# Linear attention gated by a SwiGLU block, one core: the split of the output weights in another stage, the exponentials' stores on another queue, and VectorE's scaling kept apart from GpSimd's products

## The chip, the cores and the metric

The kernel runs on one core of a Trainium2 chip. The time is the device time of one execution in microseconds (us). Three runs of the kernel before took 2455.68, 2459.19 and 2461.28 us, so the median is 2459.19 us. TensorE (PE) multiplies matrices out of SBUF into PSUM, VectorE (DVE) and ScalarE (ACT) work element by element on both memories, and GpSimd (POOL) does so on SBUF. SyncE (SP) issues the DMAs of the kernel before; each engine works through its own queue in order and waits there on semaphores.

## The reference

With x of 2048 tokens by 1024 (32 heads of 32), all in float32:

```python
xn = _layernorm(x)
# linear attention with a learned feature map
q, k, v = (xn @ wqkv), split into heads
pq, pk  = q @ w_phi, k @ w_phi                       # per head, 32 x 32
phi_q   = concat(softmax(pq), softmax(-pq))          # 64 features per head
phi_k   = concat(softmax(pk), softmax(-pk))
kv = phi_k^T v;  z = sum over tokens of phi_k
o  = (phi_q kv) / (phi_q z + 1e-6)
s  = o @ wo
# SwiGLU, 1024 -> 3584 -> 1024
g  = silu((silu(xn @ w1) * (xn @ w3)) @ w2)
out = x + s * g
```

## The kernel before, in words

Each float32 operand of a large product is split into two float32r tiles: `hi` is a cast of the source on ScalarE, `lo` is source minus `hi` on VectorE or GpSimd (`split`, L90 to L93). A product is three passes over such pairs (`PASSES`). The large products also use a seven-product scheme (`ORDER`): a pair of token tiles of 128 is taken together, and seven products of twelve matmuls each (128x128 by 128x512) give four blocks of the result; the sums of blocks that it needs are the operands A11, A12, S1 to S4, A22 for tokens and B11 to T4 for weights.

The span has these stages, with their times in the profile:

1. **Gate and up, 0 to 1141 us.** Two halves of the tokens (`tb`), 28 chunks of 128 columns of w1 and w3 each; one chunk takes about 19 us, the second half begins at about 599 us. The order of all engines is written out by hand here: `at(step, f)` puts a piece of work at a step. Beside the products of the second half the kernel prepares later weights: sums of w2's blocks (`side_w`, tile `w2o`) and the split of wo (`side_split`, L503 to L514, called at L567 to L569). wo is cut into 16 blocks of 128x512; for each, SP loads the block (256 KB), ScalarE casts, **GpSimd** subtracts (tile `wso`), and SP stores the pair to `wo_d` (512 KB).
2. **Queries, 1141 to about 1304 us** (`query_heads` L865, `query_features` L848). Eight pairs of tiles. Seven products at L874, then per tile the feature map: maximum and minimum, subtraction, and the exponential on ScalarE into one of two rooms `eq` (`e_rooms`). Each room holds both halves `c` of a tile; a half (128x1024, 512 KB) is stored to `e_d` at L863, **from SP**: four stores per pair, 32 in all. The sums give `rho` (the weights 1/sum), stored at L899.
3. **Keys and values, 1304 to 1655 us** (`heads` L800, for `c` = 1 and 2, eight pairs each). Seven products per pair at L810. ScalarE copies results out of the banks (L816 `k`, L823 and L831 `ev`), then the exponentials and kv matmuls follow. `room_ev` takes the tile `ev` from the same pool and tag (`rw`) as the two `eq` rooms: the first `ev` needs a room whose last store to `e_d` has landed. Before this stage SP also fetches the weights' sums (`fetch` L167: `op3T`, `op3B`; 2 MB each) and reloads the tokens' operands for the next pair (`reload`, L579: `xoA`, `xoS`; 512 KB each).
4. **Down-projection, 1655 to 2206 us** (`product` L1122). Seven blocks `kb` of the inner dimension by eight pairs; about 9.5 us per pair. In the last block (`kb` = 6) each finished pair also gets silu (`gate`) and its store, and the exponentials of the first tiles are loaded back (`load_e` L1079) and prepared for the last stage.
5. **Last stage, 2206 to 2454 us**, 16 tiles `t` of 128 tokens. Here too the order on all engines is that of the code. Names: `ez` = exponentials times z (`z_products` L1090, GpSimd, two halves of 128x1024); `z_sums` sums them per head (L1098, VectorE, 128x1024 to 128x32, twice) and multiplies by the weights `rho` (L1099, 128x64); `add_pairs` adds across partitions with a small matmul `us` (L1105); `factors` is the reciprocal (L1111) and a multiplication by `rho` (L1112, 128x64); `scale` multiplies the exponentials by the factors (L1119, 128x1024, per half `c`) and transposes them (L1120). Then `attend` (64 small matmuls `po`, L1252), the cast and the subtraction to `oT` (L1257, L1258), `out_half` (24 matmuls `pm` with wo, L1267, per half), and `gated` (times g on VectorE L1275, plus x on GpSimd L1276). All the small 128x64 results lie in one tile `own`, in different columns for each tile `t` (`part_of`).

Outside of the stages with a written order, and for SP in the first six blocks of stage 4, a scheduler orders the instructions by their dependences and its own priorities, so a line's place in the code doesn't fix its place in the queue.

Of the kernel before, what the change touches and what calls it, by code (L numbers as in the profile page):

```python
# [8 lines left out]
F = mybir.dt.float32  # L9
R = mybir.dt.float32r  # L10
# [7 lines left out]
P = 128  # L18
# [11 lines left out]
def tile_kernel(ctx: ExitStack, tc: tile.TileContext, x, wkT, wqT, wv, wphi, wo, w1, w3, w2, out):  # L30
# [472 lines left out]
    def side_split(d, src, s0):  # L503

        def load():
            nc.sync.dma_start(blk2(15), src)

        def do():
            t = qp.tile([P, 2, 512], R, name="wso", tag="q")
            split(t[:, 0], t[:, 1], blk2(15), nc.gpsimd)  # L510
            at(s0 + 6, lambda: nc.sync.dma_start(d, t.bitcast(F)))

        at(s0, load)
        at(s0 + 4, do)  # L514

# [332 lines left out]
    def query_features(i, j, c, p, rho, eng):  # L848
# [14 lines left out]
        nc.sync.dma_start(e_d[pairs[i][j]][:, c], ef)  # L863
# [116 lines left out]

    NEXT = ({0: 2, 1: 3, 2: 4, 3: 5, 4: 6}, {0: 2, 1: 3, 2: 4, 3: 5, 6: 6}, {})
    for c in range(3):
# [5 lines left out]
        for pos, i in enumerate(order):  # L988
            nxt, end = {}, pos + 1 == len(pairs)

            def steps():
                for j in range(7):
# [12 lines left out]
                    yield  # L1005
# [76 lines left out]
    def part_of(t, m):  # L1082
        at_ = 128 + 256 * (t % 3) + 64 * m
        return own[:, at_:at_ + 64]

    def z_products(t):
        if t >= NT:
            return
        for c in range(2):
            nc.gpsimd.tensor_mul(ezs[c].rearrange("p (g n) -> p g n", g=2), e_slab(t)[:, c].rearrange("p (g n) -> p g n", g=2),  # L1090
                                 zb[:, c * 512:c * 512 + 512].unsqueeze(1).to_broadcast([P, 2, 512]))

    def z_sums(t):
        if t >= NT:
            return
        z = part_of(t, 0)
        for c in range(2):
            nc.vector.tensor_reduce(z[:, 32 * c:32 * c + 32], ezs[c].rearrange("p (n f) -> p n f", f=DH), axis=AX.X, op=OP.add)  # L1098
        nc.vector.tensor_mul(*(v.rearrange("p (c g h) -> p c g h", c=2, g=2) for v in (z, z)), w_all[:, t])  # L1099

    def add_pairs(t, tag):
        if t >= NT:
            return
        us[t] = ps.tile([P, 512], F, name="us", tag=tag, bufs=1)[:, :64]
        nc.tensor.matmul(us[t], own[:, :P], part_of(t, 0), start=True, stop=True)  # L1105

    def factors(t):
        if t >= NT:
            return
        r, by = part_of(t, 1), part_of(t, 2)  # L1110
        nc.vector.reciprocal(r, us.pop(t))  # L1111
        nc.vector.tensor_mul(*(v.rearrange("p (c g h) -> p c g h", c=2, g=2) for v in (by, r)), w_all[:, t])  # L1112

    def scale(t, c):
        if t >= NT:
            return
        e = e_slab(t)[:, c]
        e3 = e.rearrange("p (n f) -> p n f", f=DH)
        nc.vector.tensor_mul(e3, e3, part_of(t, 2)[:, 32 * c:32 * c + 32].unsqueeze(2).to_broadcast([P, H, DH]))  # L1119
        nc.vector.transpose(et_slab(t, c), e)  # L1120
# [29 lines left out]
    FIRST = ("A11", "A12", "S2")  # L1150
    old, banks, first, second = None, {}, ready[0], None
    for r, new in enumerate(steps):
# [14 lines left out]
        for b, an, bn in TURN:  # L1167
# [26 lines left out]
        if end:  # L1194
# [7 lines left out]
            elif i == 1:  # L1202
                load_e(0)
            elif i == 2:
                load_e(1)
                z_products(0)
            elif i == 3:
                z_sums(0)
                add_pairs(0, "kv")
                z_products(1)  # L1210
            elif i == 4:
                factors(0)
                z_sums(1)
                scale(0, 0)
            elif i == 5:
                add_pairs(1, "kv")
                scale(0, 1)
                load_e(2)
            elif i == 6:
                factors(1)  # L1220
                scale(1, 0)
                load_e(3)
            elif i == 7:
                z_products(2)
# [60 lines left out]
    prev, lows = None, []  # L1285
    for t in range(NT):
        load_e(t + 4)
        p = out_half(t, 0)
# [4 lines left out]
        z_sums(t + 2)  # L1293
        z_products(t + 3)
        scale(t + 1, 1)
        gated(t, 0, p, t + 1 == NT)
        store_out(t, 0)
        add_pairs(t + 2, "us")
        lows = [attend(t + 1, 0)]
        factors(t + 2)  # L1300
        scale(t + 2, 0)
        prev = out_half(t, 1, lambda: lows.append(attend(t + 1, 1)))
        for do in lows:
            if do:
                do()
# [42 lines left out]
```

## Time and profile before

The profiled execution took 2455.37 us, with a span of 2453.6 us; the median of the runs is 2459.19 us. One execution is described by the trace; PE's granted clock was full in most of the span (0.988 on average).

| Engine | Busy, us | Share of the span |
|---|---|---|
| PE (matmuls) | 2373.6 | 97% |
| PE (weight loads, beside the matmuls) | 1941.4 | 79% |
| VectorE | 1837.6 | 75% |
| ScalarE | 854.8 | 35% |
| GpSimd | 268.5 | 11% |

PE waits for nothing in most of the span. Its gaps are in few places, and these are found by the waits of PE and by windows over stages. A row of the windows gives the stretch, its length, and for each engine the busy time with the number of instructions in brackets; then PE's granted clock, the share of the DMA engines that were busy, and the GB/s that they moved. A row of the timeline gives the start, the time, the engine, the line and what was written from what; in brackets stand the idle time of the engine before it and what ended it. A row of waits gives who waited for whom: total, times, the longest.

### The profile page before, as it was taken

The page shows a single profiled execution, that of the slowest core. Times are in us where ns is not written, and L with a number is a line of the kernel's source. Part 1 is how long each engine was busy: PE and PEld are TensorE (multiplying, and loading weights), DVE is VectorE, ACT ScalarE, POOL GpSimd, SP SyncE. Part 2 cuts the span into 40 slices and gives each one's busy share as a digit, 9 for nine tenths or more (in the row PEclk, how much of TensorE's full clock was granted, in tenths as well). Part 3 has the DMA queues.
Part 4 walks back from the last instruction along what each step waited for, and adds up shares of the span by engine and source line. Part 5 has one row for each costly group of instructions (what it writes and reads, how often), then busy time and mean ns, then how long its engine had stood idle before and what let it go on. Part 6 is the DMA issues. An engine that isn't in the chain of part 4 may idle for free.

```text
span 2453.6 us, 37229 instructions
## 1 busy us (share of the span) xinstructions
PE 2373.6 (97%) x14354; PEld 1941.4 (79%) x14354; DVE 1837.6 (75%) x2795; ACT 854.8 (35%) x1501; POOL 268.5 (11%) x233
## 2 busy tenths in 40 slices
PE   7999999999999999999997999999999999988998
PEld 6888888888888887887876888888888888766777
DVE  8877787765788888864775555575788887687996
ACT  6445454443455555532221111124322222230000
POOL 1000000000000000001331000000111111233542
PEclk9999999999999999999998999999999999998999
DMA  5446799976898988857898758644444334559662
GB/s 211 147 156 206 259 358 343 322 251 204 289 333 310 338 298 320 291 196 281 326 350 346 244 178 330 208 147 165 172 180 172 125 107 172 167 176 292 185 174 95
DMA packets 287697, 578.00 MB, mean 236 GB/s; under 512 B 24208, under 2 KB 140064, under 8 KB 284832
## 3 DMA queue, kind: packets, MB, share of 16 engines
q1 hardware_dynamic: 287520, 575.63, 68.2%
q8 instruction: 113, 1.85, 0.3%
q14 instruction: 64, 0.52, 0.1%
HBM read 370.54 MB, written 205.00 MB: 235 GB/s over the span
## 4 chain that ended last, share of the span: by engine, by line
PE 77%; DVE 12%; DMA 6%; issue 3%; ACT 1%; POOL 0%; SPq 0%; DVEq 0%; POOLq 0%; ACTq 0%
PE bankb L614 21%; PE bankb L1133 11%; PE bankc L614 10%; PE bankb L810 7%; PE bankc L1133 6%; PE banka L614 5%; PE bankc L810 3%; PE bankb L874 3%; PE banka L1133 3%; DVE acc L1119 2%; PE banka L810 2%; PE bankc L874 1%; PE pm L1267 1%; DVE own L1098 1%; DVE bo L93 1%
## 5 line engine op out<-in xcount | busy, mean ns | idle before, releaser
L93 DVE TENSOR_TENSOR bo<-rw,bo 128x512 fp32r<-128x512 f32 x336 | 234.2, 699 | 154.9 <-ACT bo L92 154.3
L92 ACT CAST bo<-rw 128x512 fp32r<-128x512 f32 x336 | 206.5, 618 | 8.4 <-DVE bo L93 2.6
L1133 PE MATMUL bankb<-bo,as 128*128 128x512 f32 x816 | 200.9, 389 | 0.0
L1133 PEld LDWEIGHTS bankb<-bo,as 128*128 128x128 f32 x816 | 153.2, 188 | 31.8
L614 PE MATMUL bankb<-op0S,bo 128*128 128x512 f32 x672 | 163.0, 391 | 1.9 <-ACT op0S L92 1.2
L1267 PE MATMUL pm<-wos,oT 128*128 128x512 f32 x576 | 145.3, 402 | 18.7 <-DVE oT L1258 16.1
L614 PE MATMUL bankc<-op0S,bo 128*128 128x512 f32 x672 | 162.5, 391 | 0.3 <-DVE op0S L93 0.3
L614 PE MATMUL bankb<-op1S,bo 128*128 128x512 f32 x672 | 161.4, 389 | 1.3 <-ACT u L649 1.3
L614 PE MATMUL bankb<-op1A,bo 128*128 128x512 f32 x672 | 158.8, 391 | 3.5 <-DVE u L657 3.1
L614 PE MATMUL bankc<-op1S,bo 128*128 128x512 f32 x672 | 161.3, 389 | 0.0
L614 PE MATMUL bankb<-op0A,bo 128*128 128x512 f32 x672 | 159.7, 391 | 0.8 <-DVE bo L93 0.5
L614 PEld LDWEIGHTS bankb<-op1A,bo 128*128 128x128 f32 x672 | 125.2, 188 | 34.0 <-DVE u L657 8.4
L1133 PE MATMUL bankc<-bo,as 128*128 128x512 f32 x576 | 150.2, 396 | 0.8 <-ACT as L92 0.7
L614 PEld LDWEIGHTS bankb<-op1S,bo 128*128 128x128 f32 x672 | 126.1, 188 | 27.9 <-ACT u L649 1.8
L614 PEld LDWEIGHTS bankb<-op0S,bo 128*128 128x128 f32 x672 | 125.2, 188 | 28.5 <-ACT op0S L92 1.6
L614 PEld LDWEIGHTS bankc<-op1S,bo 128*128 128x128 f32 x672 | 126.1, 188 | 26.2
L614 PEld LDWEIGHTS bankb<-op0A,bo 128*128 128x128 f32 x672 | 125.2, 188 | 26.9 <-DVE bo L93 0.8
L614 PEld LDWEIGHTS bankc<-op0S,bo 128*128 128x128 f32 x672 | 125.3, 188 | 26.3 <-DVE op0S L93 0.7
L1267 PEld LDWEIGHTS pm<-wos,oT 128*128 128x128 f32 x576 | 107.1, 191 | 48.8 <-DVE oT L1258 21.8
L1133 PEld LDWEIGHTS bankc<-bo,as 128*128 128x128 f32 x576 | 109.6, 191 | 25.4 <-ACT as L92 2.0
L93 POOL TENSOR_TENSOR wso<-room,wso 128x512 fp32r<-128x512 f32 x16 | 24.2, 1512 | 961.4 <-ACT wso L92 845.0
L1145 DVE TENSOR_TENSOR acc<-bankb,acc 128x512 f32<-128x512 f32 x152 | 104.1, 686 | 27.0 <-PE bankb L1133 19.8
(249 smaller groups left out, 4489.2 us busy)
## 6 DMA issues: line engine op xcount, KB each, us to landing
rw<-in_w SPq DMA_DIRECT2D x112, 512.0 KB, 4.6
hr<-h_d SPq DMA_DIRECT2D x56, 512.0 KB, 3.5
h_d<-h SPq DMA_DIRECT2D x111, 256.0 KB, 4.7
xoS<-xo_d0S SPq DMA_DIRECT2D x44, 512.0 KB, 4.9
xoS<-xo_d1S SPq DMA_DIRECT2D x44, 512.0 KB, 6.8
xoA<-xo_d0A SPq DMA_DIRECT2D x33, 512.0 KB, 3.8
xoA<-xo_d1A SPq DMA_DIRECT2D x33, 512.0 KB, 5.9
e_d<-eq SPq DMA_DIRECT2D x32, 512.0 KB, 9.2
```

Source lines behind the costliest of these rows:

```text
L92: nc.scalar.copy(hi, src)
L93: (by or nc.vector).tensor_sub(lo, src, hi.bitcast(F))
L614: nc.tensor.matmul(bank[b], bos[tb, f][bn][:, w, k], ao[an][:, u, k], start=first and n == 0, stop=LAST[b] == an and n == 11, skip_group_c ...
L810: nc.tensor.matmul(bank[b], xo[an][:, u, k], wb[bn][:, w, k], start=an in ("A11", "A12", "S1") and n == 0, stop=LAST[b] == an and n == 11, ...
L874: nc.tensor.matmul(bank[b], xo[an][:, u, k], wb[bn][:, w, k], start=an in ("A11", "A12", "S1") and n == 0, stop=LAST[b] == an and n == 11, ...
L1098: nc.vector.tensor_reduce(z[:, 32 * c:32 * c + 32], ezs[c].rearrange("p (n f) -> p n f", f=DH), axis=AX.X, op=OP.add)
L1119: nc.vector.tensor_mul(e3, e3, part_of(t, 2)[:, 32 * c:32 * c + 32].unsqueeze(2).to_broadcast([P, H, DH]))
L1133: nc.tensor.matmul(bank[b], t[:, u, pos + k], bos[kb, bn, k][:, w], start=first and n == 0, stop=LAST[b] == an and n == 5, skip_group_chec ...
L1145: nc.vector.tensor_add(c, pb, c)
L1267: nc.tensor.matmul(p, oTs[t, h][:, a, k], wos[c, 4 * h + k][:, b], start=n == 0, stop=n == 3 * ND - 1)
```

## The change

The change has three parts.

**1. The split of wo is moved** from the second half of gate and up to the keys and values. `side_split` and its 16 calls are gone. `wo_split(c, k, j, halves)` is called in `steps` for `c` = 1 and 2, once per pair and product `j`: at `j` = 0 SP loads the block into a tile of the pool `work`, at `j` = 3 ScalarE casts and **VectorE** subtracts into two more, and at `j` = 5 SP stores the two halves (256 KB each).

**2. The stores of the exponentials to `e_d`** are issued by ScalarE's queue, right behind the exponential that they store, and no more by SP.

**3. The last stage.** The 128x64 multiplications by `rho` (`weigh`, before in `z_sums`; and the second half of `factors`) go from VectorE to GpSimd. Both write to one shared column of `own`, `col(0)`, which `scale` reads: so `weigh(t + 2)` on GpSimd waits until both halves of `scale(t + 1)` on VectorE have read it, and GpSimd's `z_products(t + 3)`, queued behind, waits with it. Both halves of `scale` stand together, and both transpositions (`turn_e`) behind them. The sums of `z_sums` are separate for each half and stand behind the two subtractions to `oT`. In the last block of the down-projection a table, `pieces`, keyed by pair and product, says where the preparation of the first tiles stands; `scale(1)` and its transpositions now belong to the last stage altogether (before, its first half was done in stage 4).

How this moves instructions is seen at the end of the queries and in the last stage. SP's queue at the end of the queries (`rho_d` ends a pair; `xoA` and `xoS` are the tokens' operands for the keys; `op3T` and `op3B` the keys' weights), before:

```order
L863 DMA e_d_235<-eq 128x1024
L899 DMA rho_d<-rho 128x2x32
L167 DMA op3T_10878<-wkv_d1T_110 128x4096
L863 DMA e_d_232<-eq 128x1024
L167 DMA op3T_10905<-wkv_d1T_111 128x4096
L167 DMA op3T_10921<-wkv_d1T_112 128x4096
L167 DMA op3B_10938<-wkv_d1B_113 128x4096
L863 DMA e_d_236<-eq 128x1024
L167 DMA op3T_10964<-wkv_d1T_114 128x4096
L863 DMA e_d_232<-eq 128x1024
L863 DMA e_d_236<-eq 128x1024
L899 DMA rho_d<-rho 128x2x32
```

and after:

```order
L883 DMA rho_d<-rho 128x2x32
L563 DMA xoA_10951<-xo_d1A_94 128x1024
L563 DMA xoA_10953<-xo_d1A_95 128x1024
L563 DMA xoS_10955<-xo_d1S_96 128x1024
L563 DMA xoS_10957<-xo_d1S_97 128x1024
L167 DMA op3T_10798<-wkv_d1T_110 128x4096
L883 DMA rho_d<-rho 128x2x32
L167 DMA op3T_10825<-wkv_d1T_111 128x4096
L167 DMA op3T_10841<-wkv_d1T_112 128x4096
L167 DMA op3B_10858<-wkv_d1B_113 128x4096
L167 DMA op3T_10884<-wkv_d1T_114 128x4096
L883 DMA rho_d<-rho 128x2x32
```

The stores are out of SP's queue, and four reloads for the second pair of keys, which stood behind the last `rho_d`, now stand ahead of the four `op3T` and one `op3B`.

ScalarE's queue at the same place, after (before, the same exponentials and copies with no DMA between them); `q` is a copy of a query product, `k` and `ev` are the first copies of the keys and values:

```order
L864 COPY q<-bankc 128x512
L842 ACTIVATE eq<-eq 128x1024
L847 DMA e_d_236<-eq 128x1024
L842 ACTIVATE eq<-eq 128x1024
L847 DMA e_d_232<-eq 128x1024
L800 COPY k_10947<-bankb 128x512
L842 ACTIVATE eq<-eq 128x1024
L847 DMA e_d_236<-eq 128x1024
L807 COPY ev<-bankb 128x16x32
L115 ACTIVATE ev<-ev 128x1024
L815 COPY ev<-bankc 128x16x32
L92 CAST wo_half<-wo_raw 128x512
```

Each store stands right behind its exponential, two of them ahead of `k`'s and `ev`'s copies, and the first cast of wo behind the copies of the first pair.

VectorE's queue for one tile of the last stage, before:

```order
L1258 TENSOR_TENSOR oT<-po,oT 128x2x4x64 x2
L1275 TENSOR_TENSOR g<-pm,g 128x512
L1098 TENSOR_REDUCE own<-ez 128x32 x2
L1099 TENSOR_TENSOR own<-own,rho 128x64
L1119 TENSOR_TENSOR acc<-acc,own 128x1024
L1120 STREAM_TRANSPOSE acc<-acc 128x1024
L1275 TENSOR_TENSOR g<-pm,g 128x512
L1111 RECIPROCAL own<-us 128x64
L1112 TENSOR_TENSOR own<-own,rho 128x64
```

(the second scaling and transposition follow), and after:

```order
L1118 TENSOR_TENSOR acc<-acc,own 128x1024 x2
L1122 STREAM_TRANSPOSE acc<-acc 128x1024 x2
L1274 TENSOR_TENSOR g<-pm,g 128x512 x2
L1109 RECIPROCAL own<-us 128x64
L1257 TENSOR_TENSOR oT<-po,oT 128x2x4x64
L1095 TENSOR_REDUCE own<-ez 128x32
L1257 TENSOR_TENSOR oT<-po,oT 128x2x4x64
L1095 TENSOR_REDUCE own<-ez 128x32
```

The two 128x64 multiplications have left the queue, and the two scalings stand together. GpSimd's queue for one tile was `ez` twice and `g` twice; after, it is this (with the tiles' numbers, so that the two `ez` and the two `g` are told apart):

```order
L1100 TENSOR_TENSOR own_17950<-own_17950,rho_17949 128x64
L1090 TENSOR_TENSOR ez_17972<-acc_14211,zb_17947 128x1024
L1090 TENSOR_TENSOR ez_17973<-acc_14211,zb_17947 128x1024
L1275 TENSOR_TENSOR g_18617<-g_18617,xr_17974 128x512
L1275 TENSOR_TENSOR g_18728<-g_18728,xr_17975 128x512
L1113 TENSOR_TENSOR own_17950<-own_17950,rho_17949 128x64
```

The weighing (L1100) stands ahead of the `ez` products and holds them back, and the factors (L1113) stand behind the additions to `g`.

The diff, cut to its core:

```diff
-    def side_split(d, src, s0):
-        ...
-            split(t[:, 0], t[:, 1], blk2(15), nc.gpsimd)
-            at(s0 + 6, lambda: nc.sync.dma_start(d, t.bitcast(F)))
-        ...
-    for m in range(2 * ND):
-        c, k = divmod(m, ND)
-        side_split(wo_d[c][k], wo[k * P:(k + 1) * P, c * 512:(c + 1) * 512], HALF + 10 + 9 * m)
...
-        nc.sync.dma_start(e_d[pairs[i][j]][:, c], ef)
+        nc.scalar.dma_start(e_d[pairs[i][j]][:, c], ef)
...
+    def wo_split(c, k, j, halves):
+        if j == 0:
+            halves.append(work.tile([P, 512], F, name="wo_raw", tag="w"))
+            nc.sync.dma_start(halves[0], wo[k * P:(k + 1) * P, c * 512:(c + 1) * 512])
+        elif j == 3:
+            halves.extend(work.tile([P, 512], R, name="wo_half", tag="w") for _ in range(2))
+            split(halves[1], halves[2], halves[0])
+        elif j == 5:
+            for u in range(2):
+                nc.sync.dma_start(wo_d[c][k][:, u], halves[1 + u].bitcast(F))
...
+                    if c:
+                        wo_split(c - 1, pos, j, halves)
...
+    def col(m):
+        return own[:, P + 64 * m:P + 64 * m + 64]
...
+    def weigh(t):
+        if t < NT:
+            nc.gpsimd.tensor_mul(wide(col(0)), wide(col(1 + t % 2)), w_all[:, t])
...
+    def invert(t):
+        if t < NT:
+            nc.vector.reciprocal(col(3 + t % 2), us.pop(t))
     def factors(t):
+        if t < NT:
+            nc.gpsimd.tensor_mul(wide(col(0)), wide(col(3 + t % 2)), w_all[:, t])
     def scale(t, c):
+            nc.vector.tensor_mul(e3, e3, col(0)[:, 32 * c:32 * c + 32].unsqueeze(2).to_broadcast([P, H, DH]))
...
+    pieces = {
+        (3, 0): [lambda: z_products(0)],
+        (3, 3): [lambda: z_sums(0, 0)],
+        (3, 5): [lambda: z_sums(0, 1), lambda: weigh(0), lambda: add_pairs(0, "kv")],
+        (4, 0): [lambda: invert(0), lambda: factors(0)],
+        (4, 1): [lambda: scale(0, 0), lambda: z_products(1)],
+        (4, 4): [lambda: scale(0, 1)],
...
+        (6, 3): [lambda: invert(1), lambda: factors(1), lambda: z_products(2)],
+        (7, 2): [lambda: z_sums(2, 0)],
+        (8, 0): [lambda: z_sums(2, 1)],
+    }
...
     for t in range(NT):
         load_e(t + 4)
-        p = out_half(t, 0)
+        p, last = out_half(t, 0), t + 1 == NT
+        for c in range(2):
+            scale(t + 1, c)
+        weigh(t + 2)
+        for c in range(2):
+            turn_e(t + 1, c)
+        z_products(t + 3)
         if prev:
             gated(t - 1, 1, prev, False)
             store_out(t - 1, 1)
         load_g(t + 1)
-        z_sums(t + 2)
-        z_products(t + 3)
-        scale(t + 1, 1)
-        gated(t, 0, p, t + 1 == NT)
+        gated(t, 0, p, last)
         store_out(t, 0)
         add_pairs(t + 2, "us")
+        invert(t + 2)
+        factors(t + 2)
         lows = [attend(t + 1, 0)]
-        factors(t + 2)
-        scale(t + 2, 0)
         prev = out_half(t, 1, lambda: lows.append(attend(t + 1, 1)))
-        for do in lows:
-            if do:
-                do()
+        for c in range(2):
+            if not last:
+                lows[c]()
+            z_sums(t + 3, c)
```

More of the change, by code (lines that the diff above doesn't have):

```diff
@@ L1166, in tile_kernel @@
         bank = {}
-        for b, an, bn in TURN:
+        for m, (b, an, bn) in enumerate(TURN):
+            if kb >= NKB - 1:
+                for do in pieces.get((i if new else 8, m), ()):
+                    do()
             if an in FIRST:
@@ L1201, in tile_kernel @@
                     load_wo(k)
[L1202 to L1224, printed above, removed]
+            elif i in (1, 2, 5, 6):
+                load_e({1: 0, 2: 1, 5: 2, 6: 3}[i])
         old, banks = new, bank
```

62 lines of the change are left out of this document (25 added, 37 removed).

## The prediction

> **What bounds the kernel now.** I read the page's totals first, then the windows over the stages that the change touches, then PE's waits, and then the timeline where these are long.
>
> ```profile
> PE 2373.6 (97%) x14354; PEld 1941.4 (79%) x14354; DVE 1837.6 (75%) x2795; ACT 854.8 (35%) x1501; POOL 268.5 (11%) x233
> ...
> 627.00:993.00 366.00, 361.32 (x1580) 295.41 (x1579) 322.11 (x487) 187.07 (x347) 22.84 (x15) 1.00 0.90 314
> ...
> 1141.00:1303.70 162.70, 156.99 (x674) 127.72 (x673) 110.60 (x189) 46.32 (x56) 48.27 (x47) 0.98 0.91 344
> 1303.70:1343.00 39.30, 23.75 (x157) 18.98 (x156) 16.92 (x28) 4.72 (x6) 1.78 (x5) 0.78 1.00 401
> 1343.00:1654.70 311.70, 311.59 (x3176) 252.46 (x3174) 192.94 (x269) 62.26 (x86) 3.76 (x29) 1.00 0.65 220
> ...
> 2115.00:2206.00 91.00, 81.70 (x332) 64.58 (x330) 68.59 (x110) 33.33 (x49) 24.93 (x13) 0.92 0.58 176
> 2206.00:2240.00 34.00, 23.91 (x324) 17.03 (x324) 20.18 (x20) 3.85 (x6) 9.79 (x6) 0.80 1.03 350
> 2240.00:2418.00 178.00, 163.89 (x2191) 128.16 (x2193) 175.91 (x158) 14.12 (x24) 84.73 (x47) 1.00 0.61 175
> ...
> PE pm L1267 <- DVE oT L1258: 16.1, 12, 7.5
> PE bankb L810 <- ACT ev L823: 15.5, 1, 15.5
> ```
>
> PE is busy for 97% of the span, so only its gaps can be won. The windows show them: 4.7 us while wo is split (627 to 993); 5.7 us in the queries; 15.6 us at the start of the keys, one wait for a copy on ScalarE; none in the rest of the keys and values; 9.3 us in the last block of the down-projection; 10 us where the last stage starts; 14 us in its steady part. In that part alone another engine is full: VectorE is busy for 175.91 of 178 us.
>
> **Part 1: the split of wo.**
>
> ```profile
> L92 ACT CAST wso<-room x16: 613/620/622, 639.6 to 1016.6; 128x512 fp32r<-128x512 f32 x16
> L93 POOL TENSOR_TENSOR wso<-room,wso x16: 1291/1528/1830, 640.3 to 1017.3; 128x512 fp32r<-128x512 f32 x16
> ...
> 640.58 2.66 PE L614 MATMUL banka<-op1A,bo 128*128 128x512 f32 x11
> ...
> 991.41 1.75 PE L614 MATMUL banka<-op1A,bo 128*128 128x512 f32 x7
> ...
> 1010.46 1.75 PE L614 MATMUL banka<-op1A,bo 128*128 128x512 f32 x7
> ```
>
> These are PE's rows at the same place of a chunk. From 991.41 to 1010.46 a chunk takes 19.05 us; the 18 chunks from 640.58 to 991.41 take 350.8 us, or 19.49 each, so 8 us more than 18 undisturbed ones. The sixteen subtractions on GpSimd run in just these chunks, at 1.5 us each beside VectorE's. The gain is between 0 (another side job makes the gap) and 8 us; PE's idle time there is 4.7 us, so I take +5.
>
> In the keys and values, the sixteen blocks come back: on ScalarE 16 x 0.62 = 9.9 us beside 62 of 312 us; on VectorE 16 subtractions, at about 0.7 us (the 128x512 forms on VectorE, L1275 below), 11 us beside 193. Per pair SP issues three DMAs more (one of 256 KB in, two out), 12 MB over a stage that keeps the DMA engines at 0.65. All three have room, and PE had no gap at all there. What is queued behind a cast is a copy out of a bank, which PE waits for. If every cast were on the path it would cost 9.9 us; if none, 0. A cast is short beside the 2.7 us of one product, so I take -1.
>
> **Part 2: the stores on ScalarE's queue.**
>
> ```profile
> 1303.93 0.38 SPq L167 DMA_DIRECT2D op3T<-wkv_d1T  x1
> ...
> 1307.65 3.32 SPq L863 DMA_DIRECT2D e_d<-eq  x2
> ...
> 1309.57 1.06 ACT L858 ACTIVATE eq<-eq 128x1024 f32<-128x1024 f32 x1 [1.47 <-issue]
> ...
> 1313.28 0.37 SPq L899 DMA_DIRECT2D rho_d<-rho  x1
> ...
> 1329.91 0.59 ACT L823 COPY ev<-bankb 128x512 f32<-128x512 f32 x1 [19.28 <-DMA rho_d<-rho]
> ...
> 1330.55 4.82 PE L810 MATMUL bankb<-op3T,xoS 128*128 128x512 f32 x12 [15.55 <-ACT ev L823]
> ...
> op3T<-wkv_d1T SPq DMA_DIRECT2D x4, 2048.0 KB, 13.7
> ...
> SPq L863 <- ACT eq L858: 69.8, 23, 5.5
> ...
> SPq L863 <- DMA op3B<-wkv_d1B: 7.2, 2, 3.7
> ...
> SPq L863 <- DMA xoA<-xo_d1A: 4.3, 5, 1.4
> ```
>
> The copy to `ev` waits 19.28 us, until 1329.91. The view names the DMA of `rho_d`; but `ev` takes a room of `eq`, so it is the landing of the last stores to `e_d` that frees it. They are issued at about 1307.7 and 1310.7, behind five fetches of 2 MB that take 13.7 us each while the DMA engines are full (1.00, 401 GB/s), and on the same queue. In the window PE's clock is also low (0.78), and the twelve matmuls behind the wait take 4.82 us where twelve took 2.7 in gate and up (2.66 for eleven, above): 2.1 us more. So 15.5 + 2.1 = 17.6 us is all that can be won here.
>
> With the stores on ScalarE's queue, SP no longer stands 69.8 us at L863 waiting for exponentials, so the fetches are issued earlier, and the last two stores are in a queue of their own. If both queues share the DMA engines evenly, 512 KB at half of 401 GB/s take 2.6 us; with the exponential ending at 1310.63 the room is free by about 1316 and ScalarE is late by a microsecond or so, not 15. Nothing in this trace shows two queues at once. The ends: 0, if the stores wait behind the fetched bytes as before, and 17.6. What would be late next is the last `op3T`: 2 MB more of reloads stand ahead of it now, some 5 us at 401 GB/s, but SP gets to it earlier. Its product stands about 5 us behind the one that waits. I take +16, near the upper end, since the copy and no fetch is what ends the gap in this trace.
>
> The Trainium skill, in "DMA: Bandwidth & Descriptors", section "Issuing engines are not separate DMA queues", says that DMAs run on the same 16 engines whichever engine started them, and that several issuers save only the time to issue. By that sentence alone the stores would land no sooner, and this term is 0. The same page's section "Queues, rings and completion order" has each DMA engine take packets from the queues in turn, and by that the store gets its half. No run here shows which.
>
> The price is in ScalarE's queue. An issue takes it 0.3 to 0.4 us (SP's single issues above: 0.38, 0.37), four per pair 1.5 us, beside 46 us of work in 163. But the two rows of SP at L863 that wait for other DMAs (7.2 and 4.3 us) would now stand on ScalarE, and behind them the exponentials and the copies of the banks, for which PE waits. The ends: -11.5, if all of it reaches PE, and +5.7, if reloads come earlier by SP's freed time and PE's whole gap goes. I take -2.
>
> **The last block of the down-projection.** The same products, sums and scalings stand at other places. One scaling and one transposition leave, and the two sums of tile 2 come in; VectorE has 68.6 of 91 us. PE's 9.3 us of gaps there may go or double: -9.3 to +9.3, and since nothing speaks for one more than for the other I take 0.
>
> **Part 3: the last stage.**
>
> ```profile
> L1119 DVE TENSOR_TENSOR acc<-acc,own x32: 1197/1226/3424, 2158.4 to 2425.8; 128x1024 f32<-128x1024 f32 x32
> ...
> L1099 DVE TENSOR_TENSOR own<-own,rho x16: 209/1520/2048, 2152.3 to 2415.6; 128x64 f32<-128x64 f32 x16
> ...
> L1112 DVE TENSOR_TENSOR own<-own,rho x16: 209/946/1005, 2155.7 to 2419.3; 128x64 f32<-128x64 f32 x16
> ...
> L1120 DVE STREAM_TRANSPOSE acc<-acc x32: 1225/1245/1246, 2162.2 to 2427.0; 128x1024 f32<-128x1024 f32 x32
> ...
> L1098 DVE TENSOR_REDUCE own<-ez x32: 1196/1202/1219, 2148.2 to 2414.4; 128x32 f32<-128x1024 f32 x32
> ...
> L1111 DVE RECIPROCAL own<-us x16: 539/541/547, 2154.7 to 2418.7; 128x64 f32<-128x64 f32 x16
> ...
> L1275 DVE TENSOR_TENSOR g<-pm,g x32: 651/672/692, 2229.9 to 2449.0; 128x512 f32<-128x512 f32 x32
> ...
> L1090 POOL TENSOR_TENSOR ez<-acc,zb x32: 2372/2390/3402, 2145.4 to 2402.2; 128x1024 f32<-128x1024 f32 x32
> ...
> L1276 POOL TENSOR_TENSOR g<-g,xr x30: 1267/1290/2207, 2232.8 to 2438.9; 128x512 f32<-128x512 f32 x30
> ...
> 2311.36 4.72 POOL L1090 TENSOR_TENSOR ez<-acc,zb 128x1024 f32<-128x1024 f32 x2
> ...
> 2312.32 1.52 DVE L1099 TENSOR_TENSOR own<-own,rho 128x64 f32<-128x64 f32 x1
> ...
> 2313.76 3.41 DVE L1119 TENSOR_TENSOR acc<-acc,own 128x1024 f32<-128x1024 f32 x1
> ...
> 2241.67 0.33 PE L1105 MATMUL us<-own 128*128 128x64 f32 x2
> ...
> 2254.93 0.33 PE L1105 MATMUL us<-own 128*128 128x64 f32 x2
> ...
> 2417.29 0.33 PE L1105 MATMUL us<-own 128*128 128x64 f32 x2
> ```
>
> The timeline of one tile shows the mechanism: while `ez` runs on GpSimd (2311.36 to 2316.08), the small multiplication takes 1.52 us where it needs 0.21, and the scaling 3.41 where it needs 1.23: it ends 1.1 us after `ez` does. The transpositions and sums, which read one tile, keep their time (at most 1246 and 1219 ns).
>
> The period is the distance of the `us` matmuls. From 2241.67 to 2254.93 a tile takes 13.26 us, with VectorE still ahead; from 2254.93 to 2417.29, eleven tiles take 162.36, or 14.76 each. After the change VectorE has per tile 2 x 1.23 (scaling) + 2 x 1.245 + 2 x 0.67 (`g`) + 0.54 (reciprocal) + 2 x 0.67 (`oT`, the size of `g`)  + 2 x 1.20 = 10.6 us, since 1.52 + 0.95 leave its queue and 2.2 of the scaling's 3.4 go. That is under 13.26, so PE is the bound again: 11 x (14.76 - 13.25) = +16.6 us.
>
> GpSimd's new loop has to fit as well. `weigh` waits for the scaling; behind it on GpSimd stand `ez` twice (4.8), `g` twice (2.6) and `factors`, for which the next scaling waits. No row shows a 128x64 multiplication on GpSimd. A line through 128x512 (1.29) and 128x1024 (2.39) gives about 0.3 us; it is not above 1.29, nor below 0. With 0.33 each the loop is 2.5 (two scalings) + 0.3 + 4.8 + 2.6 + 0.3 = 10.5 us, with 1.29 each 12.5; both are under 13.26. `add_pairs` on PE waits for `weigh`, but stands half a tile later. So +16.6, at least +11 if the waits between the three engines cost 0.5 us a tile, at most +17.
>
> At its start PE waits 7.5 us for `oT` of tile 1, because VectorE stands at `g` until g has been loaded. Now the subtraction to `oT` comes right behind the reciprocal, ahead of sums; but a scaling and a transposition (1.23 + 1.25) are added there. Ends -2.5 and +7.5; I take +2.
>
> **The sum.** +5 - 1 + 16 - 2 + 0 + 16.6 + 2 = 36.6 us. From the profiled 2455.4 that is 2418.8; this execution was 3.8 us under the median of 2459.2, so on the median's scale 2422.
>
> **The rivals.**
>
> *The stores land no sooner.* For it: the DMA engines are full there, and the last stores are issued no earlier, at 1307.7 and 1310.7. Against it: the fetches ahead of them start earlier. The term of 16 goes: 2459.2 - 20.6 = 2438.6. I give it 0.17. The sentence of the Trainium skill on issuing engines, in "DMA: Bandwidth & Descriptors", section "Issuing engines are not separate DMA queues", says the same.
>
> *The loop through GpSimd becomes the bound of the last stage.* It decides from 14.76 us a tile on, for which each small multiplication would have to take 2.4 us; or the hand-over PE, VectorE, GpSimd, VectorE costs about a microsecond at each step. Then the 16.6 go: 2439. For it: POOL's `g` waits for VectorE and stands ahead of `factors`. 0.12.
>
> *Slower: ScalarE's queue stands at its DMA issues.* SP's waits at L863 for exponentials vanish on ScalarE, but a wait for an earlier DMA stops the exponentials and copies behind it. To turn the sign it must take 41 us from PE over eight pairs, 5.1 each, or about 1.3 us at each of the 32 stores. The rows give 11.5 us of such waits on SP in seven cases (longest 3.7), so it needs about four times that. At 1.5 us a store 48 us are lost: 2459.2 - 36.6 + 48 = 2470. 0.1.
>
> *Scaling and `ez` aren't kept apart*, if `weigh` is late enough to put `ez` on the next tile's scaling: this excludes itself, since `factors` stands behind `ez` in one queue. It needs no chance.
>
> **How the numbers follow.** The forecast has 0.57, the two rivals with a smaller gain 0.17 and 0.12, the slower one 0.1, and 0.04 is left for losses that just cancel. Of the forecast's cases a few lie under 2409 (all terms near their upper ends: 8 + 17.6 + 0 + 3 + 17 + 4 = 50). So 2409 to 2442 takes in the forecast and both smaller gains and leaves out some 0.18. A measurement of this kernel can tell 0.2% (5 us) from no change: faster 0.86, same 0.04, slower 0.1.
>
> **What would show it.** Right: `us` rows 13.3 us apart, all scalings at about 1.23 us, the first `ev` copy of the keys waiting under 4 us with the store landing in some 5 us, no gap between 627 and 993, and none in the keys and values. Wrong: waits of the `q` copies or exponentials behind a DMA on ScalarE and PE's idle time above 6 us in the queries; POOL's small multiplications above 2 us; a wait of PE for `ev` as long as before.

## The result, and the profile after

The changed kernel takes 2420.39 us (median of four runs, 2417.87 to 2423.55) against 2457.43 us of the kernel before, measured beside it (four runs, 2453.52 to 2461.28). The ratio is 0.985, with a 95% interval of 0.9829 to 0.9871: 37 us less. The profiled execution took 2423.55 us with a span of 2421.8, so it was the slowest of the four, while that of before (2455.37) lies at the low end of its runs. Between the two traces only 31.8 us can be found.

The page's totals and the windows over the same stages, after (columns as before: busy time and count of PE, its weight loads, VectorE, ScalarE, GpSimd; clock; DMA share; GB/s):

```profile
PE 2366.6 (98%) x14354; PEld 1941.1 (80%) x14354; DVE 1770.9 (73%) x2779; ACT 856.9 (35%) x1501; POOL 253.4 (10%) x249
...
1135.20:1299.20 164.00, 157.05 (x674) 127.92 (x673) 112.95 (x189) 47.59 (x56) 48.68 (x47) 0.98 0.97 364
1299.20:1338.00 38.80, 31.07 (x186) 24.48 (x185) 21.39 (x35) 7.51 (x10) 1.49 (x5) 0.91 0.90 356
...
627.00:993.00 366.00, 365.14 (x1606) 300.70 (x1605) 314.34 (x495) 182.56 (x339) 0.00 (x0) 1.00 0.85 289
2102.00:2194.00 92.00, 81.75 (x336) 63.54 (x335) 68.32 (x107) 33.38 (x49) 27.07 (x17) 0.96 0.61 185
2194.00:2228.00 34.00, 24.57 (x331) 17.51 (x331) 15.34 (x17) 3.77 (x6) 8.31 (x7) 0.90 1.01 336
2228.00:2386.00 158.00, 158.00 (x2171) 127.92 (x2170) 119.94 (x135) 14.12 (x24) 93.42 (x73) 1.00 0.69 191
```

The gap in gate and up is closed (365.14 of 366 us busy, before 361.32). The start of the keys still has 7.7 us without a matmul, before 15.6. In the steady part of the last stage PE has no gap at all, and VectorE is down from 176 of 178 us to 120 of 158.

PE's waits of the changed kernel, the last store but one to `e_d` and the copy to `ev` that waited for its landing, and of the last stage the rows of the operations that the prediction spoke of:

```profile
PE bankb L794 <- ACT ev L807: 6.5, 1, 6.5
PE pm L1266 <- DVE oT L1257: 6.0, 1, 6.0
PE bankb L1135 <- ACT af L92: 5.0, 2, 2.6
PE bankb L858 <- DMA xoA<-xo_d0A: 4.4, 1, 4.4
...
1302.86 0.33 ACTq L847 DMA_DIRECT2D e_d<-eq  x1
...
1316.03 0.59 ACT L807 COPY ev<-bankb 128x512 f32<-128x512 f32 x1 [10.24 <-DMA e_d<-eq]
...
L1118 DVE TENSOR_TENSOR acc<-acc,own x32: 1210/1216/1459, 2144.3 to 2392.7; 128x1024 f32<-128x1024 f32 x32
...
L1100 POOL TENSOR_TENSOR own<-own,rho x16: 322/325/702, 2140.2 to 2382.1; 128x64 f32<-128x64 f32 x16
...
L1113 POOL TENSOR_TENSOR own<-own,rho x16: 314/336/639, 2142.2 to 2387.7; 128x64 f32<-128x64 f32 x16
...
2228.04 0.33 PE L1105 MATMUL us<-own 128*128 128x64 f32 x2
2241.16 0.33 PE L1105 MATMUL us<-own 128*128 128x64 f32 x2
2385.48 0.33 PE L1105 MATMUL us<-own 128*128 128x64 f32 x2
```

The scalings take 1.2 us, at most 1.46 (before up to 3.42). The period of a tile is (2385.48 - 2241.16) / 11 = 13.12 us, before 14.76.

Each stage begins with its first matmul; the differences of these starts give where the time went in the two traces:

| Stage | Before, us | After, us | Gain | Predicted |
|---|---|---|---|---|
| up to the queries (start at 1141.4, 1135.2) | 1141.4 | 1135.2 | +6.2 | +5 |
| queries (to 1304.0, 1299.2) | 162.6 | 164.0 | -1.4 | -2 |
| keys and values (to 1654.7, 1642.8) | 350.7 | 343.6 | +7.1 | +16 - 1 |
| down-projection (to 2206.1, 2194.0) | 551.4 | 551.2 | +0.2 | 0 |
| last stage to the `us` of the fourth tile | 35.6 | 34.0 | +1.5 | +2 |
| `us` of the fourth tile to that of the last | 175.6 | 157.4 | +18.2 | +16.6 |
| from there to the end | 36.3 | 36.3 | 0 | 0 |

Six terms are within 1.6 us of the forecast. One is not: the gap at the start of the keys gave half of what was forecast.

### The profile page after: what moved, and what is told of

The parts are those of the page before. It is cut to its first block, busy times and chain, and to the rows that moved or that the text cites. A ratio compares the mean times of both kernels' runs of the same rounds, so it can differ in the third digit from the quotient of the medians.

```text
span 2421.8 us, 37223 instructions
## 1 busy us (share of the span) xinstructions
PE 2366.6 (98%) x14354; PEld 1941.1 (80%) x14354; DVE 1770.9 (73%) x2779; ACT 856.9 (35%) x1501; POOL 253.4 (10%) x249
## 4 chain that ended last, share of the span: by engine, by line
PE 46%; DMA 4%; DVE 1%; ACT 0%; issue 0%; SPq 0%; ACTq 0%
PE bankb L1135 12%; PE bankb L794 7%; PE pm L1266 7%; PE bankc L1135 6%; PE bankc L794 4%; PE banka L1135 3%; PE bankb L858 2%; PE banka L794 2%; DMA xoS<-xo_d1S 2%; PE bankc L858 1%; PE pkv L779 1%; PE po L1251 1%; DMA acc<-e_d 1%; DMA g_d<-acc 1%; PE banka L858 0%; DMA wos<-wo_d 0%
## 5 line engine op out<-in xcount | busy, mean ns | idle before, releaser
L1135 PEld LDWEIGHTS bankb<-bo,as 128*128 128x128 f32 x816 | 153.2, 188 | 31.8
L839 POOL TENSOR_TENSOR eq<-q,mm 128x512 f32<-128x512 f32 x24 | 25.3, 1052 | 1209.7 <-DVE mm L837 1113.7
```

The source lines that it names most:

```text
L839: eng.tensor_sub(e[:, 0], p3, mm[:, 0, :].unsqueeze(2).to_broadcast([P, 16, DH]))
L1135: nc.tensor.matmul(bank[b], t[:, u, pos + k], bos[kb, bn, k][:, w], start=first and n == 0, stop=LAST[b] == an and n == 5, skip_group_chec ...
```

## The experiments

### Each part alone, and the changed kernel without part 2

Three kernels have one part of the change each, on the kernel before: the wo split moved, the stores issued by ScalarE's queue, or the last stage. A fourth is the changed kernel with

```diff
-        nc.scalar.dma_start(e_d[pairs[i][j]][:, c], ef)
+        nc.sync.dma_start(e_d[pairs[i][j]][:, c], ef)
```

> The kernel before with part 1 alone (wo split in the keys and values, subtraction on VectorE). Theory (the loss in gate and up comes from the split, and the keys have room for it): the second half of gate and up ends 5 to 6 us earlier, the keys and values have the same length within 1 us, total 5 to 6 us less than before. Rival (another side job makes the gaps, or the casts cost the keys what gate and up gain): total within 2 us of before.

> The kernel before with part 2 alone (e_d stores issued by ScalarE's queue). Theory: the first wait of the keys for ev falls from 15.5 to some 6 us, as in the changed kernel, and the queries get 1 to 2 us longer: total 7 to 9 us less. Rival (the stores land no sooner by themselves, the gain there came with the moved wo work): wait still above 13 us, total within 2 us of before.

> The kernel before with part 3 alone (the last stage and its preparation). Theory: the last stage takes 13.1 us a tile in place of 14.76 and starts 1 to 2 us earlier, total 19 to 20 us less. Rival (part of the gain comes from the other parts, as by the clock that PE has left after shorter gaps): 13.3 us a tile or more, or total less than 16 us below.

> The changed kernel with the stores to e_d issued by SP again, the rest unchanged. Theory (the queue is what shortens the gap): the wait for ev is back at 14 to 17 us, total 7 to 9 us over the changed kernel. Rival (the order of fetches and reloads is what shortens it): wait at 6 to 8 us, total within 2 us of the changed kernel.

| Kernel | us | Ratio to before (95%) | Wait for ev | Keys and values | Period of a tile |
|---|---|---|---|---|---|
| part 1 alone | 2450.11 | 0.9968 (0.9957 to 0.998) | 13.9 | 348.9 | 14.75 |
| part 2 alone | 2446.83 | 0.9962 (0.9948 to 0.9975) | 6.5 | 342.5 | 14.76 |
| part 3 alone | 2436.32 | 0.9913 (0.99 to 0.9927) | 14.6 | 350.3 | 13.12 |
| after, stores by SP | 2428.87 | 0.9886 (0.9873 to 0.99) | 14.3 | 349.7 | 13.12 |

The ratios are worth 7.9, 9.3 and 21.4 us, 38.6 together against 37 measured: the parts add up within their intervals (each some 3 us either way), and no effect of one part on another is seen. In the fourth kernel 8.5 us come back. Its edit also changes SP's order: the four reloads stand behind the last `rho_d` again, and the first fetch is issued 8.8 us ahead of the keys, not 16.1. So this run alone doesn't part the queue from the order. The changed kernel's trace does: the store issued by ScalarE at 1302.86 landed by 1316.0, together with a fetch of `op3B` that SP had issued 8 us earlier (1294.84, 21.0 us to landing), and SP's queue went on with packets of over 8 KB behind it (38 from 1316 to 1318 us). The store had not stood behind these fetches. With the stores by SP, the last two were issued at 1300.30 and 1303.30, and the `ev` copy started only at 1321.26. For part 3 the rival is out: the period is the same without the other parts. Part 1 gave somewhat more than expected; the trace has 3.9 us of it up to the queries (1137.5 against 1141.4) and 1.8 in the keys, 1.6 of these by a shorter wait for `ev`; the rest lies within the runs' spread.

### Why gate and up lost time to the split

```diff
-            split(t[:, 0], t[:, 1], blk2(15), nc.gpsimd)
+            split(t[:, 0], t[:, 1], blk2(15))
```

on the kernel before: the same load, cast and store at the same place, the subtraction on VectorE.

> The kernel before with the subtraction of the wo split on VectorE in place of GpSimd, at its old place in gate and up. Theory (GpSimd's 1.5 us subtractions hold up VectorE's there): gate and up end 4 to 7 us earlier, total 4 to 7 us less than before. Rival (the place is at fault: the load, the cast or the store crowd the stage, or VectorE is full with the 11 us more): gate and up end at 1139 us or later, total within 2 us of before.

Measured: 2451.92 us, ratio 0.9979 (0.997 to 0.9987), or 5.2 us less. VectorE's costliest groups from 640 to 993 us, first of the kernel before (its window over the stage stands in the prediction), then this one's window from 627 to 993 and its groups:

```profile
L93 DVE TENSOR_TENSOR bo<-rw,bo 128x512 fp32r<-128x512 f32 x110 | 79.0, 719 | 37.3 <-ACT bo L92 37.1
L93 DVE TENSOR_TENSOR w2o<-room,w2o 128x512 fp32r<-128x512 f32 x105 | 74.5, 715 | 0.4 <-ACT w2o L92 0.4
```

```profile
627.00:993.00 366.00, 365.29 (x1605) 300.41 (x1604) 320.05 (x505) 189.85 (x351) 0.00 (x0) 1.00 0.91 318
...
L93 DVE TENSOR_TENSOR bo<-rw,bo 128x512 fp32r<-128x512 f32 x112 | 76.9, 688 | 34.7 <-ACT bo L92 34.0
L93 DVE TENSOR_TENSOR w2o<-room,w2o 128x512 fp32r<-128x512 f32 x105 | 71.2, 684 | 0.9 <-ACT w2o L92 0.9
```

VectorE does fifteen of the sixteen subtractions more in this window and is busy for 320 us where it was 322: its other subtractions take 688 and 684 ns on average in place of 719 and 715, and PE's gap falls from 4.7 to 0.7 us. In this window it was GpSimd's subtraction beside VectorE's that cost the time, not the split's place. The end of the stage says less: in this trace the queries start at 1140.8 us, only 0.6 earlier than before, which is the rival's sign. Of the 4.0 us that the window gained, 1.1 had been lost by the start of the second half (600.9 against 599.8) and 2.4 went in a gap of PE between 600 and 627 us, ahead of the first block of wo. The total decides for the theory: 3.2 to 7.4 us less by its interval. Part 1 gave 4.9 to 10.6, so a good part of its gain was to be had without moving the split; how much moving it adds is not settled.

### What is left at the start of the keys

Two kernels on the changed one. The first gives the first pair's two `ev` tiles room in two weights' operands that are free by then (`home` is 5 and 6 for them, and None afterwards), so that no store has to land:

```diff
-        t = rwp.tile([P, 2048], F, name="ev", tag="rw")
+        if home is None:
+            t = rwp.tile([P, 2048], F, name="ev", tag="rw")
+        else:
+            t = big.tile([P, 2, 4, 512], F, name="ev", tag=f"big{home}")
+            t = t.rearrange("p u k t -> p (u k t)")[:, :2048]
```

> The changed kernel, where the first pair of keys takes its two ev tiles from places of the weights' operands (big5 and big6) that are free by then, so that no store to e_d has to land first. Theory (the 6.5 us that are left at the start of the keys are the landing of a store): the wait of PE for ev goes, the keys and values take 337 to 339 us in place of 343.6, total 4 to 7 us under the changed kernel (2414 to 2417). Rival (a fetched operand of the keys lands just behind it, and PE waits for that): wait for op3T of 4 us or more, total within 2 us of the changed kernel.

The second cuts the fetches into pieces of 4 KB:

```diff
-            nc.sync.dma_start(t.bitcast(F), wkv_d[m - 2][n])
+            if m == 3:
+                for w in range(2):
+                    for k in range(0, 4, 2):
+                        nc.sync.dma_start(t[:, w, k:k + 2].bitcast(F), wkv_d[1][n][:, w, k:k + 2])
+            else:
+                nc.sync.dma_start(t.bitcast(F), wkv_d[m - 2][n])
```

> The changed kernel with each fetch of the first keys' weights cut into four DMAs that move 4 KB pieces in place of 16 KB ones; same bytes. Theory (the two queues take turns by piece, so a queue of 4 KB stores beside one of 16 KB fetches gets a fifth of the bytes; 3.15 of 15.6 MB in the changed kernel's window): the stores land in 6 to 9 us in place of 12 to 13, the wait for ev falls to 0 to 3 us, if no fetched operand is late by it. Rival (the share doesn't hang on the size of the pieces): stores at 11 to 13 us, wait at 6 to 7.

Own rooms: 2413.06 us, ratio 0.9816 (0.9803 to 0.983); keys and values 337.4 us. 4 KB pieces: 2412.84 us, 0.9822 (0.9808 to 0.9835); keys and values 338.1 us. Both are some 7 us under the changed kernel, and PE's wait for `ev` is gone or 1.9 us; 1.6 us each of waits for two fetched operands take its place with the own rooms, 1.9 for one with the pieces. So the 6.5 us were the landing of a store, and the fetches would not have allowed much more.

Why the stores took so long shows in the DMA view, for 1304 to 1310 us: all packets, then packets, MB and share of the 16 engines' time by queue (q1 is SP's, q10 ScalarE's). The changed kernel first, then that with 4 KB pieces:

```profile
DMA packets 283, 2.58 MB, mean 429 GB/s; under 512 B 32, under 2 KB 32, under 8 KB 157
...
q1 hardware_dynamic: 141, 2.05, 79.8%
q10 hardware_dynamic: 141, 0.51, 21.2%
```

```profile
DMA packets 683, 2.52 MB, mean 419 GB/s; under 512 B 72, under 2 KB 72, under 8 KB 682
...
q1 hardware_dynamic: 399, 1.47, 59.8%
q10 hardware_dynamic: 283, 1.03, 42.3%
```

In the changed kernel both queues moved 141 packets, SP's of 2.05 MB / 141 = 14.5 KB on average, ScalarE's of 3.6 KB (32 packets under 512 B are counted in). In the 6 us ahead of these it was 142 to 140, and in the 6 us behind them 139 to 142. The queues take turns by the packet, so the bytes go four to one. The Trainium skill, in "DMA: Bandwidth & Descriptors", section "Queues, rings and completion order", says that each engine goes round its queues a packet at a time; the trace agrees, with 141 packets to 141. With small pieces the stores' share of the bytes doubles, and stores land in 8.7 us at most, in place of 13.1. There the packets were 399 to 283 and not one to one; why SP's queue got more turns in that run is not shown.

As a control, the fetches were cut by partitions: as many DMAs as with 4 KB pieces, but pieces of 16 KB.

```diff
+                for q in range(4):
+                    nc.sync.dma_start(t[32 * q:32 * q + 32].bitcast(F), wkv_d[1][n][32 * q:32 * q + 32])
```

> The changed kernel with each fetch of the first keys' weights cut into four DMAs of 32 partitions: as many DMAs as in the run with 4 KB pieces, but each piece still 16 KB. Theory (the share of the queues goes by the size of the pieces): stores land in 11 to 13 us, the wait for ev stays at 5 to 7 us. Rival (more and shorter DMAs hold SP's queue back, and that made room for the stores): stores at 8 us, wait 2 us as with the 4 KB pieces.

2438.95 us, ratio 0.9922 (0.9907 to 0.9937): 18.6 us more than the changed kernel. PE's wait for `ev` is gone here too, and the stores land in 7.5 us at the median, which is what the rival said. But the weights are late:

```profile
1294.57 24.85 SPq L169 DMA_DIRECT2D op3T<-wkv_d1T  x11
...
PE bankb L798 <- DMA op3T<-wkv_d1T: 7.8, 2, 3.9
...
PE bankc L798 <- DMA op3B<-wkv_d1B: 5.3, 1, 5.3
...
DMA packets 332, 1.75 MB, mean 292 GB/s; under 512 B 54, under 2 KB 54, under 8 KB 282
...
q10 hardware_dynamic: 250, 0.93, 48.0%
q1 hardware_dynamic: 82, 0.82, 47.5%
```

SP took 24.85 us to issue eleven fetches and 34.3 for all twenty; with 4 KB pieces all twenty took 21.3. In the same 6 us as above its queue moved 82 packets. The DMA engines were busy for nearly all of it (48.0% and 47.5% of their time), but moved 292 GB/s in place of 429, so the packets themselves took longer; why is not shown. This run can't serve as a control, since it changes both the issuing and the rate of the transfers. How much of their gain is the size of the pieces, and how much the held queue, stays open; the turns by the packet are read from the changed kernel itself.

### Which part of the last stage's change carries it

The changed kernel with a column of its own for `weigh`, so that GpSimd no longer waits for the scaling:

```diff
-            nc.gpsimd.tensor_mul(wide(col(0)), wide(col(1 + t % 2)), w_all[:, t])
+            nc.gpsimd.tensor_mul(wide(col(5)), wide(col(1 + t % 2)), w_all[:, t])
...
-            nc.tensor.matmul(us[t], own[:, :P], col(0), start=True, stop=True)
+            nc.tensor.matmul(us[t], own[:, :P], col(5), start=True, stop=True)
```

> The changed kernel with weigh in a column of its own, so that GpSimd waits no more for the scaling; the multiplications stay on GpSimd. Theory (keeping them apart is needed): ez runs on GpSimd while VectorE scales again, one or both scalings take 2.3 to 3.4 us, VectorE has 12.8 to 15.0 us of work per tile and the period is 13.5 to 15 us, total 4 to 20 us over the changed kernel. Rival (to move the two small multiplications was enough): scalings slow, but the period stays at 13.1 us since PE still bounds it, total within 2 us.

The changed kernel with both multiplications on VectorE (`nc.vector` for `nc.gpsimd` in `weigh` and `factors`):

> The changed kernel with weigh and the multiplication of factors on VectorE again, in the new order of the last stage. Theory (the new order is enough: with both scalings directly behind the sums, VectorE is ahead of GpSimd's ez there and GpSimd waits, as in the run with two columns): period 13.1 us, total within 3 us of the changed kernel. Rival (the two multiplications have to leave VectorE, since one stands under ez): 1.5 to 2 us of weigh and up to 2.2 of a scaling come back, period 13.6 to 14.8 us, total 6 to 18 us over.

The kernel before with both multiplications on GpSimd (`nc.gpsimd` for `nc.vector` in `z_sums` and `factors`), nothing else moved:

> The kernel before with the two 128x64 multiplications on GpSimd and nothing else moved. Theory (it is these multiplications and what they let GpSimd start first): VectorE has 10.6 to 12.8 us of work, period 13.1 to 13.4 us, total 14 to 18 us under the kernel before. Rival (the order of the scalings is needed too): the wait of VectorE for factors, which stand behind ez and g on GpSimd, takes their place, period 14 to 15 us, total within 8 us of before.

| Kernel | us | Ratio to before (95%) | Period, us |
|---|---|---|---|
| two columns | 2419.33 | 0.9841 (0.9826 to 0.9856) | 13.12 |
| after, multiplications on VectorE | 2422.58 | 0.985 (0.9834 to 0.9867) | 13.28 |
| before, multiplications on GpSimd | 2448.56 | 0.9961 (0.9947 to 0.9976) | 14.03 |

Two columns cost nothing, against the theory. Its timeline shows why (one tile):

```profile
2311.71 2.48 DVE L1118 TENSOR_TENSOR acc<-acc,own 128x1024 f32<-128x1024 f32 x2
2311.93 1.17 POOL L1100 TENSOR_TENSOR own<-own,rho 128x64 f32<-128x64 f32 x1 [3.47 <-DVE own L1095]
2313.06 3.39 POOL L1090 TENSOR_TENSOR ez<-acc,zb 128x1024 f32<-128x1024 f32 x1
```

GpSimd now starts while VectorE scales, but just behind it, and it is mostly GpSimd that pays (the scalings keep 1218 ns at the median, 2835 at most): 1.17 us for `weigh` (0.33 alone), which ends with the first scaling, and 3.39 for the first `ez` (2.4 alone), which begins under the second, while the two scalings take their 2.48 us. In these rows the engine that starts first keeps its pace. The Trainium skill, in "SBUF — State Buffer", section "Who interferes with whom", says that the order of issue decides who is blocked; the trace agrees, with 3.41 us for a scaling behind `ez` (before) and 1.2 for one ahead of it. The shared column isn't what keeps the scalings fast; by the timeline it is that they stand directly behind the sums, for which GpSimd waits as well (3.47 us <-DVE own L1095). No run moves the scalings alone, so within the new order this step is read from the trace and not tested by itself.

With the multiplications on VectorE some scalings come under `ez` again, but there is room for it:

```profile
L1118 DVE TENSOR_TENSOR acc<-acc,own x32: 1215/1329/3424, 2142.7 to 2394.1; 128x1024 f32<-128x1024 f32 x32
...
L1100 DVE TENSOR_TENSOR own<-own,rho x16: 217/224/225, 2138.3 to 2383.4; 128x64 f32<-128x64 f32 x16
...
L1113 DVE TENSOR_TENSOR own<-own,rho x16: 217/356/1540, 2141.9 to 2388.2; 128x64 f32<-128x64 f32 x16
```

The two small multiplications take 0.22 and 0.36 us at the median, before 1.52 and 0.95: in the new order they hardly meet `ez`. Of the 1.64 us a tile, 1.48 are had by the new order without the other engine, and 0.16 by the other engine. In the old order, the other engine makes a new wait:

```profile
  POOL own L1112: 51.6, 14
...
2317.93 0.32 POOL L1112 TENSOR_TENSOR own<-own,rho 128x64 f32<-128x64 f32 x1
2318.28 1.23 DVE L1119 TENSOR_TENSOR acc<-acc,own 128x1024 f32<-128x1024 f32 x1 [4.12 <-POOL own L1112]
```

The scalings are fast here too (1218 ns at the median), but VectorE waits 51.6 us in 14 times for the factors, which stand behind `ez` and `g` on GpSimd. Theory and rival were each half right, and the period falls half the way.

### A version that is faster than both

The own rooms, and in the first tile of the last stage the multiplication by g behind the two subtractions to `oT` (the second piece stands behind the loop over `lows` and `z_sums`):

```diff
-        gated(t, 0, p, last)
-        store_out(t, 0)
+        if t:
+            gated(t, 0, p, last)
+            store_out(t, 0)
...
+        if not t:
+            gated(t, 0, p, last)
+            store_out(t, 0)
```

> The changed kernel with the two ev tiles of the first pair of keys in free places (as in the run with own rooms), and in the first tile of the last stage the multiplication by g behind the two subtractions to oT, so that VectorE doesn't stand at a g that is not loaded while PE waits for oT. Theory: the wait of PE for oT (6.0 us) falls under 2 us on top of the 7 us of the own rooms, total 2406 to 2409 us. Rival (g's late load holds up PE in another place, by the banks pm or GpSimd's queue): total within 2 us of the kernel with own rooms alone, 2413.

2410.13 us (2407.37 to 2414.63), ratio 0.9807 (0.9791 to 0.9822). That is 47 us under the kernel before and 10 under the changed one. Against the own rooms alone, 0.9816, the step in the first tile is not clear of the spread, and the total lies between what the theory and the rival said. Its trace shows a part of each theory:

```profile
2207.09 0.69 DVE L1279 TENSOR_TENSOR g<-pm,g 128x512 f32<-128x512 f32 x1 [5.96 <-DMA g<-g_d]
...
2211.97 0.43 PE L1110 MATMUL us<-own 128*128 128x64 f32 x2 [3.69 <-POOL own L1105]
```

PE's wait for `oT` is gone, but VectorE still stands 5.96 us at `g`, the scalings of the next tile behind it, and PE waits 3.69 us for `weigh`, which they hold back.

## Why the prediction was right, and where it wasn't

The total, its direction and its range held: 2420.4 us against 2422, within 2409 to 2442. That the sum came so near to the difference of the medians (36.6 against 37) is in part luck: one of its terms was 8 us too large, the two traces differ by 31.8, and the runs of one kernel spread over 6 to 8 us.

- **Part 1, +5 and -1.** Right in size (+6.2 in the traces), and so was GpSimd's subtraction as the row to look at (fifteen of the sixteen, not all, lie in the 18 chunks that were compared; the last starts at 1017.3 us). That the keys have room held: without their first wait they take 337.1 us after (343.6 - 6.5), 336.0 with part 2 alone and 335.2 before, so the split costs 1 to 2 us there.
- **Part 2, +16.** The mechanism was right: `ev` waits for a store, not for `rho_d`, and the queue of its own shortens that. The size was wrong. The step that failed is "if both queues share the DMA engines evenly, 512 KB at half of 401 GB/s take 2.6 us". The queues share by packets, and SP's were four times as large: 0.51 of 2.56 MB went to the stores. At a fifth of 401 GB/s one store takes 6.5 us, and a store stood behind others of its own queue, which the prediction's price left out: issued at 1298.73, 1302.86 and 1305.82, the second took 13.1. In place of 16 the term measured 8.2 us (keys and values 350.7 and 342.5, part 2 alone).
- **ScalarE's queue, -2.** -1.4 in the traces of the whole change, +1.6 with part 2 alone: about nothing. ScalarE's waits there name a DMA four times, 14.7 us in all (3.4 before), more than the 11.5 that the prediction feared, but PE's largest wait for one of its copies is 2.4 us. PE's idle time in the queries is 7.0 us, above the 6 that were named as a sign of being wrong; 4.4 of it are a wait for the load of `xoA`, 3.1 before. The rival that ended slower found no ground.
- **The last block of the down-projection, 0.** +0.2.
- **Part 3, +16.6 and +2.** +18.2 and +1.5. PE is the bound as forecast, and GpSimd's small multiplications take 0.33 us as estimated from a line through two rows. The period is 13.12 and not 13.25, 0.13 us less than the one tile of before from which it was taken. The reason given was right only in part. The scaling under `ez` was priced as what the change avoids by keeping the engines apart; the runs show that giving up the shared column costs nothing, and that the new order does nearly all.
- **The signs.** The `us` rows, the scalings and the window from 627 to 993 came as forecast. The `ev` copy did not: it waited 10.24 us in place of under 4, and its store took 13.1 in place of some 5.
- **The rival that the stores land no sooner** is refuted by the kernel with SP's stores (14.3 against 6.5 us) with the landing times, though half of its price was there. The loop through GpSimd as a bound is refuted by 13.12 us, but it does appear where the old order is kept (14.03).

## What to carry to other kernels

Where two engines hinder each other, ask which of them starts first: an order that lets the critical engine start first was worth as much here as keeping them apart, and moving work to the other engine can put it behind that engine's long operations, as with the old order (51.6 us of waits). A store on a queue of its own doesn't wait for the fetches ahead of it, but beside a queue of larger packets it gets only the share that its packets have; a wait for its landing goes away altogether with another room. Check a sum term by term on the trace, for a total within 2 us of its forecast held a term that was wrong by 8.

## What the runs showed of the hardware

Two DMA queues moved 141 packets each in 6 us, 2.05 MB and 0.51 MB; with 4 KB pieces on both it was 399 to 283. A 128x64 multiplication on GpSimd took 0.33 us, and 1.17 when VectorE's scaling had begun before it; a 128x1024 `ez` 2.4 and 3.39. Cutting five fetches of 2 MB into four DMAs each by partitions held SP's queue for 34.3 us over the twenty issues, and the kernel took 18.6 us more than the changed one; as many DMAs over all partitions held it for 21.3 us, and the kernel took 7.6 us less.
